# Cross network kernel, last layer: two residual additions made by accumulating GpSimd transfers onto the output, and two groups of loads made one load each

## The chip, the cores and the metric

The kernel runs on one core of a Trainium2 chip. The metric is the device time of one execution in microseconds (us), a median over several executions. The engines are called by the profile's names: PE (TensorE), DVE (VectorE), ACT (ScalarE), POOL (GpSimd) and SP (SyncE). A name with a q behind it (SPq, POOLq) is an engine's instruction queue, where DMAs are issued and semaphores are waited for.

## The reference

```python
B, D, L = 4096, 416, 6            # bf16 throughout
def reference(x0, ws, bs):        # x0 [B, D], ws [L, D, D], bs [L, D]
    x = x0
    for l in range(L):
        x = x0 * (x @ ws[l] + bs[l]) + x
    return x
```

Each of the six layers is a 4096 x 416 by 416 x 416 product, a bias, a product by element with x0 (below: the multiply) and a sum with the layer's own input (below: the add).

## The kernel before

**Layers 0 to 4** keep x transposed: features lie on the partitions, batch columns along the free axis. 416 features are three blocks of 128 (tiles XM) and a rest of 32 (tiles XR). The 4096 columns are two halves, s = 0 and 1, each of four groups of 512. PE writes into PSUM, ACT evacuates a tile of 1024 columns and adds the bias (L163), DVE multiplies by x0 (L164) and adds x (L167).

**The last layer** (from L313) swaps the operands: 128 batch rows are the stationary side, so the result comes out as rows and can be stored as it lies. For it the kernel keeps x0 as rows (X0rows, loaded by SP at L123) and the layer's input as rows (XLrows). XLrows is made near the end of layer 4 by six transposing transfers of SP (L203) for the three blocks and two ACT copies (L276) for the rest. The bias row is loaded to partitions 0, 32, 64 and 96 of bLr (L125), and a one-row matmul of ones by bLr (L334) adds it in PSUM.

The 32 row blocks of 128 rows are worked off in four rounds of eight units, a unit being one row block (L360 to L380). A round has two "quads" q and q + 1 of four units, g = 0 to 3; unit (q, g) is row block 16 s + 4 g + i, where quad q stands for (s, i). The rounds are q = 0, 2, 4 and 6. Below, u0 to u7 are the eight units of the last round: u0 to u3 are (6, 0) to (6, 3), and u4 to u7 are (7, 0) to (7, 3). For each unit PE makes three matmuls (L325) and a share of L331 and L334. The function `ew` (L345) then has

- ACT cast the PSUM result to bf16 in a tile t (L352; `tpool`, 6 buffers),
- DVE multiply t by the X0rows block in place (L353),
- the add of the unit before it done by `close_sum` (L339): DVE writes t + XLrows to a tile o (L342; `opool`, 10 buffers), and o is stored (L343),
- its own add put in the list `pending`.

So DVE's order, fixed by `keep_in_program_order`, is multiply of unit n, add of unit n - 1, multiply of unit n + 1, add of unit n, and so on. In rounds 0 and 2 and for the first pair of round 4, two row blocks go through as one instruction of 832 columns; all the other units are single, 416 columns. Stores go through SP's queue, except that of the last unit, u7, which ACT issues (L367).

POOL issues no DMA in this kernel. It fills constants and copies weights and a piece of x0 near the start (L95 to L133), and then has nothing to do. SP issues the early loads in the order of L98 to L125: the transposed x0, the weights, the four X0rows loads (L123, 832 KB each) and the four bLr loads (L125, 0.8 KB each).

Of the kernel before, what the change touches and what calls it, by code (L numbers as in the profile page):

```python
# [10 lines left out]
ALU = mybir.AluOpType  # L11
# [5 lines left out]
def kernel(  # L17
# [7 lines left out]
    nc = tc.nc  # L25
    B, D = x0.shape
    L = ws.shape[0]
    P = 128
# [4 lines left out]
    NG = 4  # L33
# [3 lines left out]
    LL = L - 1  # L37
# [7 lines left out]
    x0_v = x0.rearrange("(bt p) d -> p bt d", p=P)  # L45
    out_v = out.rearrange("(bt p) d -> p bt d", p=P)
# [8 lines left out]
    bLr = const.tile([P, D], BF16)  # L55
    bM = const.tile([P, NK, L], FP32)
    bR = const.tile([P, L], FP32)
    X0rows = big.tile([P, NBT, D], BF16)
    XLrows = big.tile([P, NBT, D], BF16)
# [10 lines left out]
    def load_wm(eng, l):  # L70
        eng.dma_start(WM[:, l], ws[l, 0:NK * P, :].rearrange("(k p) n -> p k n", p=P))
# [33 lines left out]
    for g in range(1, NG):  # L105
        dst, src = WR[32 * g:32 * g + 32, 0, :], WR[0:R, 0, :]
# [12 lines left out]
        load_wr(nc.sync, g, 1, L)  # L119
    for l in range(2, L):  # L120
        load_wm(nc.sync, l)
    for q in range(4):
        nc.sync.dma_start(X0rows[:, 8 * q:8 * q + 8, :], x0_v[:, 8 * q:8 * q + 8, :])  # L123
    for g in range(NG):
        nc.sync.dma_start(bLr[32 * g:32 * g + 1, :], bs[LL:LL + 1, :])  # L125

    def fill_wd(l0, l1):
        for g in range(NG):
# [186 lines left out]
    NQ = len(quads)  # L315
# [23 lines left out]
    def close_sum():  # L339
        while pending:  # L340
            o, t, xl, dst, eng = pending.pop()
            tc.keep_in_program_order(nc.vector.tensor_tensor(out=o, in0=t, in1=xl, op=ALU.add))  # L342
            eng.dma_start(dst, o)  # L343

    def ew(q, g0, n, src, eng):  # L345
        s, i = quads[q]
        b0 = 16 * s + 4 * g0 + i
        b = slice(b0, b0 + 4 * (n - 1) + 1, 4)
        t = tpool.tile([P, 2 * CW], BF16, name="t")
        o = opool.tile([P, 2, D], BF16, name="o")  # L350
        tv = t[:, 0:n * D].rearrange("p (a d) -> p a d", a=n)
        nc.scalar.copy(tv, src)  # L352
        tc.keep_in_program_order(nc.vector.tensor_tensor(out=tv, in0=tv, in1=X0rows[:, b, :], op=ALU.mult))  # L353
        close_sum()
        pending.append((o[:, 0:n, :], tv, XLrows[:, b, :], out_v[:, b, :], eng))
# [5 lines left out]
    for q, at, done in rounds:  # L361
        tiles = [psum.tile([P, 2, CW], FP32, tag="ps", name=f"py{n}") for n in range(4)]
        bank = [tiles[n][:, a, :] for n, a in at]

        def close(u, n):
            tl, a = at[u]
            ew(q + u // 4, u % 4, n, tiles[tl][:, a:a + n, 0:D], nc.scalar if q + 2 == NQ and u == 7 else nc.sync)  # L367

        for u in range(done):
            mm_q_full(q, u, bank[u], False)  # L370
        mm_q_rem(q, bank[0:4], done)
        close(0, done)
        mm_q_rem(q + 1, bank[4:8], 0)
        for u in range(done, 8):
            mm_q_full(q + u // 4, u % 4, bank[u], True)
            if at is not PAIRS:
                close(u, 1)
            elif u % 2:
                close(u - 1, 2)
# [31 lines left out]
```

## Time and profile before

| | |
|---|---|
| device time, median of 3 runs | 130.65 us (130.53 to 130.75) |
| the profiled execution's own time | 130.58 us |
| span of the profiled execution, first to last instruction | 128.8 us |
| granted TensorE clock | 1.000 |
| PE, DVE, ACT, POOL busy | 123.6, 106.7, 86.9, 6.2 us |
| last round: first and last matmul (start) | 119.7 and about 124.2 us |
| last round: first multiply and last add (start) | 121.20 and 125.81 us |
| issue of the last store (L343 on ACTq) | 126.22 us |

All places in time are microseconds from the span's start. "Idle before" in a row is the idle time of the engine ahead of the instruction, with what ended it. Consecutive DVE instructions overlap in the rows: the add of a single unit lasts 0.37 us, but the next instruction starts 0.28 to 0.29 us after it, and that distance is what one instruction costs when DVE has work waiting.

### The profile page before, as it was taken

How to read it: one execution, taken by the hardware profiler on the slowest of the kernel's cores; microseconds unless marked ns; L12 is line 12 of the kernel's file. 1: busy time of each engine (PE TensorE's matmuls, PEld its weight loads, DVE VectorE, ACT ScalarE, POOL GpSimd, SP SyncE). 2: the span in 40 equal slices, each digit the busy share in tenths (PEclk: the TensorE clock that was granted, in tenths of full speed). 3: DMA queues.
4: the chain of work that ended last, by engine and by line, in shares of the span. 5: the costliest groups of instructions: out<-in, count | busy, mean ns of one | idle time of the engine just before them, and what ended most of it. 6: DMA issues, size and time to landing. Idle time of an engine off the chain costs nothing.

```text
span 128.8 us, 3973 instructions
## 1 busy us (share of the span) xinstructions
PE 123.6 (96%) x1691; PEld 55.1 (43%) x1691; DVE 106.7 (83%) x195; ACT 86.9 (67%) x99; POOL 6.2 (5%) x18
## 2 busy tenths in 40 slices
PE   7999999999999999999999999999999999999960
PEld 3343443344545444434444544444444445445420
DVE  0023989999999898989898989898989899898991
ACT  0138873887848667848668848668858896569670
POOL 4004300600000000000000000000000000000000
PEclk9999999999999999999999999999999999999999
DMA  4999999999990000000000000000297999985754
GB/s 95 244 231 207 163 153 264 253 328 333 336 291 9 5 0 8 0 0 5 0 5 0 5 0 5 0 5 0 45 163 169 119 237 191 217 261 186 235 178 138
DMA packets 42102, 16.37 MB, mean 127 GB/s; under 512 B 30906, under 2 KB 42084, under 8 KB 42084
## 3 DMA queue, kind: packets, MB, share of 16 engines
q1 hardware_dynamic: 39368, 15.53, 53.9%
q10 hardware_dynamic: 2716, 0.59, 2.5%
q8 instruction: 13, 0.21, 0.7%
q14 instruction: 5, 0.04, 0.1%
HBM read 6.15 MB, written 3.41 MB: 74 GB/s over the span
## 4 chain that ended last, share of the span: by engine, by line
PE 89%; DVE 6%; issue 2%; ACT 1%; DVEq 0%
PE pt L179 49%; PE ph L212 13%; PE py L325 8%; PE pt L185 5%; PE pr L196 5%; PE wps L139 4%; DVE t L353 4%; DVE o L342 2%; PE pr L191 2%; PE ph L219 1%; PE py L331 1%; PE py L334 1%; ACT t L352 1%; PE tpr L155 0%; PE pr L155 0%
## 5 line engine op out<-in xcount | busy, mean ns | idle before, releaser
L179 PE MATMUL pt<-XM,WM 128*32 128x512 bf16 x1152 | 65.2, 379 | 0.0
L163 ACT ACTIVATE t<-pt,bM 128x1024 bf16<-128x1024 f32 x48 | 49.6, 1115 | 18.5 <-PE pt L185 18.5
L164 DVE TENSOR_TENSOR t<-t,XM 128x1024 bf16<-128x1024 bf16 x60 | 41.4, 690 | 5.2 <-ACT t L163 5.2
L167 DVE TENSOR_TENSOR XM<-t,XM 128x1024 bf16<-128x1024 bf16 x60 | 41.8, 697 | 3.4
L179 PEld LDWEIGHTS <-WM 128*32 128x32 bf16 x1152 | 29.7, 97 | 33.8 <-issue 5.1
L352 ACT CAST t<-py 128x416 bf16<-128x416 f32 (+1 forms) x23 | 14.8, 642 | 4.8 <-PE py L325 2.6
L325 PE MATMUL py<-WM,XM 128*128 128x416 bf16 x96 | 17.7, 340 | 0.0
L212 PE MATMUL ph<-XM,WM 128*128 128x512 bf16 x72 | 16.5, 381 | 0.0
L163 ACT ACTIVATE t<-ph,bM 128x1024 bf16<-128x1024 f32 x12 | 12.5, 1114 | 3.4 <-PE ph L219 3.4
L325 PEld LDWEIGHTS <-XM 128*128 128x128 bf16 x96 | 9.0, 98 | 8.5 <-issue 1.4
L353 DVE TENSOR_TENSOR t<-t,X0rows 128x416 bf16<-128x416 bf16 (+1 forms) x23 | 10.4, 457 | 1.2 <-ACT t L352 1.2
L342 DVE TENSOR_TENSOR o<-t,XLrows 128x416 bf16<-128x416 bf16 (+1 forms) x23 | 10.4, 456 | 0.0
L212 PEld LDWEIGHTS <-WM 128*128 128x128 bf16 x72 | 6.7, 98 | 8.4 <-issue 1.1
L171 ACT ACTIVATE t<-pr,bR 128x512 bf16<-128x512 f32 x10 | 6.4, 685 | 2.7 <-PE pr L196 2.1
L196 PE MATMUL pr<-XM,WM 128*32 128x512 bf16 x120 | 8.2, 379 | 0.0
L185 PE MATMUL pt<-XR,WR 32*128 32x512 bf16 x96 | 7.3, 379 | 0.0
L139 PE MATMUL wps<-const-bfloat16-1.0 128*128 128x512 bf16 (+1 forms) x12 | 4.9, 592 | 0.8 <-PEq L395 0.8
L104 ACT ACT_TABLE_LOAD x1 | 1.3, 1283 | 6.0 <-DMA XM<-in_x_dram 6.0
L173 DVE TENSOR_TENSOR XR<-t,XR 128x512 bf16<-128x512 bf16 x10 | 4.2, 425 | 0.7
L196 PEld LDWEIGHTS <-WM 128*32 128x32 bf16 x120 | 3.2, 97 | 3.0
L150 DVE CAST bM<-pb 128x18 f32<-128x18 bf16 x1 | 0.2, 177 | 5.1 <-PE pb L149 5.1
L172 DVE TENSOR_TENSOR t<-t,XR 128x512 bf16<-128x512 bf16 x10 | 4.2, 420 | 0.0
(38 smaller groups left out, 33.5 us busy)
## 6 DMA issues: line engine op xcount, KB each, us to landing
X0rows<-in_x_dram SPq DMA_DIRECT2D x4, 832.0 KB, 11.5
out_dram<-o SPq DMA_DIRECT2D x9, 208.0 KB, 2.5
WM<-in_ws_dram SPq DMA_DIRECT2D x5, 312.0 KB
out_dram<-o SPq DMA_DIRECT2D x13, 104.0 KB, 1.9
WR<-in_ws_dram SPq DMA_DIRECT2D x4, 130.0 KB, 4.1
WM<-in_ws_dram ACTq DMA_DIRECT2D x1, 312.0 KB
XM<-in_x_dram SPq DMA_TRANSPOSE x8, 4.9
xrig<-in_x_dram ACTq DMA_DIRECT2D x4, 32.0 KB, 4.2
```

What stands on the lines that cost most here:

```text
L139: nc.tensor.matmul(wps[:, 0:cols], lhsT=warm[:, 0:P], rhs=warm[:, 0:cols], start=True, stop=True)
L163: nc.scalar.activation(t[:], pt[:].rearrange("p a b -> p (a b)"), ACT.Identity, bias=bM[:, m, l:l + 1], scale=1.0)
L164: prod = nc.vector.tensor_tensor(out=t[:], in0=t[:], in1=XM[0][:, m, c0:c0 + 2 * CW], op=ALU.mult)
L167: nc.vector.tensor_tensor(out=nxt[:, m, c0:c0 + 2 * CW], in0=t[:], in1=cur[:, m, c0:c0 + 2 * CW], op=ALU.add)
L179: nc.tensor.matmul(pts[g // 2][32 * q:32 * q + 32, g % 2, :], lhsT=WM[:, l, k, 128 * m + 32 * q:128 * m + 32 * q + 32], rhs=cur[:, k, c0:c ...
L185: nc.tensor.matmul(pts[g // 2][:, g % 2, :], lhsT=WR[32 * g:32 * g + 32, l, 128 * m:128 * m + 128], rhs=curR[32 * g:32 * g + 32, CW * s:CW ...
L196: nc.tensor.matmul(pr[32 * g:32 * g + 32, :], lhsT=WM[:, l, k, NK * P:D], rhs=cur[:, k, c0:c0 + CW], start=False, stop=(k == NK - 1), tile ...
L212: nc.tensor.matmul(pt[:, gl, :], lhsT=WM[:, 0, k, 128 * m:128 * m + 128], rhs=cur[:, k, c0:c0 + CW], start=(k == 0 and not after_row), sto ...
L325: nc.tensor.matmul(py[:, 0:D], lhsT=cur[:, k, q_cols(q, g)], rhs=WM[:, l, k, :], start=((not closes) and k == 0), stop=(closes and k == NK ...
L342: tc.keep_in_program_order(nc.vector.tensor_tensor(out=o, in0=t, in1=xl, op=ALU.add))
L352: nc.scalar.copy(tv, src)
L353: tc.keep_in_program_order(nc.vector.tensor_tensor(out=tv, in0=tv, in1=X0rows[:, b, :], op=ALU.mult))
```

## The change

There are two edits.

1. **Loads.** The four X0rows loads become one load of the whole tile, and the four bLr loads become one load to partitions 0, 32, 64 and 96 from the broadcast bias row. Both stay on SP's queue at the same place.
2. **Two sums.** For the units u1 and u2 of the last round, (6, 1) and (6, 2), POOL stores the XLrows row block to the output by itself; POOL's queue gets these two transfers before the last layer's rounds are emitted. When the unit comes up, DVE's multiply writes its product to o and not back to t, and POOL issues a transfer of o to the same output rows with `accum_op=add`. The unit has no add on DVE, and no store on SP's queue; it isn't put in `pending`.

```diff
-    for q in range(4):
-        nc.sync.dma_start(X0rows[:, 8 * q:8 * q + 8, :], x0_v[:, 8 * q:8 * q + 8, :])
-    for g in range(NG):
-        nc.sync.dma_start(bLr[32 * g:32 * g + 1, :], bs[LL:LL + 1, :])
+    nc.sync.dma_start(X0rows[:], x0_v)
+    nc.sync.dma_start(bLr[0:P:32, :], bs[LL:LL + 1, :].to_broadcast([NG, D]))
...
-    def ew(q, g0, n, src, eng):
+    def rows_of(q, g0, n):
         s, i = quads[q]
         b0 = 16 * s + 4 * g0 + i
-        b = slice(b0, b0 + 4 * (n - 1) + 1, 4)
+        return slice(b0, b0 + 4 * (n - 1) + 1, 4)
+
+    ADDED = ((NQ - 2, 1), (NQ - 2, 2))
+    for q, u in ADDED:
+        b = rows_of(q, u, 1)
+        nc.gpsimd.dma_start(out_v[:, b, :], XLrows[:, b, :])
+
+    def ew(q, g0, n, src, eng):
+        b = rows_of(q, g0, n)
         t = tpool.tile([P, 2 * CW], BF16, name="t")
         o = opool.tile([P, 2, D], BF16, name="o")
         tv = t[:, 0:n * D].rearrange("p (a d) -> p a d", a=n)
         nc.scalar.copy(tv, src)
+        if (q, g0) in ADDED:
+            tc.keep_in_program_order(nc.vector.tensor_tensor(out=o[:, 0:n, :], in0=tv, in1=X0rows[:, b, :], op=ALU.mult))
+            nc.gpsimd.dma_start(out_v[:, b, :], o[:, 0:n, :], accum_op=ALU.add)
+            close_sum()
+            return
```

## The prediction

> **What bounds the kernel now.** I read the chain of work that ended last first, then the timeline of the last round, engine by engine. The page's shares of the chain say that PE carries it:
>
> ```profile
> PE 123.6 (96%) x1691; PEld 55.1 (43%) x1691; DVE 106.7 (83%) x195; ACT 86.9 (67%) x99; POOL 6.2 (5%) x18
> ...
> PE 89%; DVE 6%; issue 2%; ACT 1%; DVEq 0%
> ```
>
> But the change touches no PE work; what it may win lies where the chain is not PE. In order of time that is the stretch from 115.67 us on, DVE almost alone, and it ends so:
>
> ```profile
> 124.67 0.34 DVE t L353
> 125.02 0.09 issue
> 125.10 0.02 DVEq L342
> 125.12 0.12 issue
> 125.24 0.37 DVE t L353
> 125.62 0.29 DVE o L342
> 125.90 0.28 DVEq L406
> ```
>
> The timeline of ACT and then of DVE for the last round (start, duration) shows who feeds whom:
>
> ```profile
> 121.28 3.67 ACT L352 CAST t<-py 128x416 bf16<-128x416 f32 x7 [0.47 <-PE py L325]
> ...
> 121.82 0.38 DVE L353 TENSOR_TENSOR t<-t,X0rows 128x416 bf16<-128x416 bf16 x1
> 122.11 0.37 DVE L342 TENSOR_TENSOR o<-t,XLrows 128x416 bf16<-128x416 bf16 x1
> 122.40 0.37 DVE L353 TENSOR_TENSOR t<-t,X0rows 128x416 bf16<-128x416 bf16 x1
> ...
> 125.24 0.37 DVE L353 TENSOR_TENSOR t<-t,X0rows 128x416 bf16<-128x416 bf16 x1
> 125.53 0.66 DVE L342 TENSOR_TENSOR o<-t,XLrows 128x416 bf16<-128x416 bf16 x2
> ```
>
> The seven casts are u1 to u7. Each is 0.506 us, so their starts lie (3.67 - 0.506) / 6 = 0.527 us apart and the last ends at 124.95. DVE's multiply of u1 starts at 121.82, 0.03 after its cast ended (121.28 + 0.506 = 121.79): there DVE has just caught up with ACT. That of u7 starts at 125.24, 0.29 after its cast: DVE falls behind, because a multiply and an add cost (125.24 - 121.82) / 6 = 0.57 us a unit, 0.285 an instruction, against 0.527 from ACT. So the end of the round is set by DVE, but **ACT, with PE ahead of it, is only 0.04 us a unit faster**. PE works without a gap over 0.1 us until some 124.4, and ACT waits for nothing after 121.28.
>
> Behind the last add (start 125.81) come the store of u7 and its landing:
>
> ```profile
> 126.22 0.37 ACTq L343 DMA_DIRECT2D out_dram<-o  x1
> ...
> L406 SPq DRAIN x3: 7/7/13, 128.0 to 128.4; - x3
> ```
>
> SP has seen all stores land at 128.0, so the last takes about 1.8 us from its issue (the rows of L343 have 1.7 to 2.5 from issue to landing); the closing barrier ends the span at 128.8.
>
> **Part 1, the merged loads: nothing.** The four X0rows issues hold SP's queue from 23.28 for 7.84 us and the four bLr issues from 31.16 for 3.35 us. SP's next work is the first transposing transfers of layer 4, at 91.5 us for L203; the longest wait there is 58.2 us. The first reader of bLr is PE at 105.0, that of X0rows is DVE at 107.43, and the loads land by about 28.6 + 11.6 = 40 us. Were one load to take twice the whole stretch it would still be 40 us early, and as it is behind all other loads it can delay none. A gain is excluded as well, since SP would only wait longer.
>
> **Part 2, DVE.** Two adds go, 2 x 0.285 = 0.57 us of DVE work, but only what lies behind the last empty moment of DVE shortens the end. I walk the new order with casts ending at 121.28 + 0.527 (n - 1) + 0.506 for unit n and 0.03 us to the multiply:
> - multiply u1 121.82, add u0 122.11, multiply u2 122.40 (cast ready at 122.34): as before.
> - No add of u1. Multiply u3 waits for its cast, 122.84 + 0.03 = 122.87 (before: 122.97).
> - No add of u2, and that of u3 stands behind multiply u4. DVE idles until u4's cast, 123.37 + 0.03 = 123.40 (before: 123.54).
> - From there eight instructions follow without a gap (add u3, multiply u5, add u4, multiply u6, add u5, multiply u7, add u6, add u7): the last starts at 123.40 + 8 x 0.285 = 125.68 instead of 125.81.
>
> So **0.13 us are gained, not 0.57**: the lag before u4, three units of 0.043 us. The other 0.44 us become DVE waiting for ACT. Even an infinitely fast add ahead of u7 would leave multiply u7 at 124.98 and its add at 125.27, a gain of 0.54 us: that is the limit for any change on DVE alone.
>
> **Part 2, POOL.** Four DMA issues are new on a queue that has issued none. The first two need XLrows of half 1: the last transposing transfer is issued at 107.5 and lands 6.0 us later, 113.5. Two issues and a landing have no row on POOL. From below: the shortest store issue, 0.33 us, and 1.7 to land; from above: the longest issue of an early load, 2.48, and 2.7, the longest landing of a store. That is 113.5 + 2 x 2.48 + 2.7 = 121.2 at the latest, still before the accumulating transfers, which wait for these.
>
> The products of u1 and u2 are done at 121.82 + 0.38 = 122.20 and 122.77. The second accumulating issue stands behind the first on POOL's queue; nothing else is queued there. With an issue of g and a landing of h it is down at 122.20 + 2 g + h. With the bounds that is 124.56 (0.33, 1.7) to 129.86 (2.48, 2.7); the limit is 128.0 - 0.13 = 127.9, when the store of u7 lands. I take g = 1.14, the longest issue of a store at L343, and h = 2.5: 126.98, **0.9 us before it is needed**. So I cost it at nothing; u7's store covers it, and past g = 1.6 (with h = 2.5) it sets the end. By the Trainium skill (DMA: Bandwidth & Descriptors, Anatomy of one DMA) a GpSimd transfer of 106 KB would take 2.0 + 0.24 us, an estimate that puts it further inside; no run here shows it for an accumulating one.
>
> What else falls away: two stores on SP's queue, which kept pace with DVE anyway (SP waits for DVE ahead of nearly every one). What else is added: about 0.2 MB of stores and the accumulating traffic, at a DMA share of 0.42 to 0.68 from 114 us on; u7's store could land a little later, between 0 and 0.8 us (2.5 instead of 1.7). I take 0. At the close POOL's queue has a DRAIN of at most 0.83 us in the rows; it lies beside u7's landing.
>
> Sum against the profiled execution's own time: 130.58 - 0.13 = 130.45. That execution is 0.07 under the median, so on the median it is **130.5 us**.
>
> **Rivals.**
> (a) **POOL's transfers end last (slower).** An issue may not get on while DVE works. The traces have POOL and DVE side by side only near the start, and there they get in each other's way:
>
> ```profile
> 14.90 0.68 DVE L164 TENSOR_TENSOR t<-t,XM 128x1024 bf16<-128x1024 bf16 x1
> 15.62 0.98 DVE L167 TENSOR_TENSOR XM<-t,XM 128x1024 bf16<-128x1024 bf16 x1
> ...
> 15.00 1.06 POOL L132 COPY xrig<-xrem 128x512 bf16<-128x512 bf16 x1 [3.65 <-DMA xrem<-in_x_dram]
> ```
>
> If the accumulating issues had to wait until DVE's last add is over, 126.05, they would land at 126.05 + 2 x 0.33 + 1.7 = 128.4 up to 126.05 + 2 x 1.14 + 2.5 = 130.8, 0.5 to 2.9 us behind 127.9: 130.9 to 133.4 on the median; by the middle some 132. The point from which it decides is 127.9 us for the second landing. Slow issues alone (g = 2.48) come to 129.86, 132.5 on the median. Against it: DVE is idle in the new order before u3 and u4, just when the first issue starts. The Trainium skill (SBUF — State Buffer, two separate sides) has this as a trap: GpSimd can't write descriptors while DVE runs a 2-port mode. Its section Who interferes with whom says that an addition of two SBUF operands has no such mode and is in the way of GpSimd's reads only, inferred for descriptors. The row above, a POOL copy that reads, agrees with the second; no row shows the first. Chance 0.27.
>
> (b) **DVE is slowed by POOL (slower).** The same rows: DVE's 0.69 became 0.98 beside a POOL copy of 1.06 us; two others, beside L129's copies, took 0.80 and 0.81. If issues act likewise between 122.2 and 124.5, the instructions from multiply u4 on that fall in it (four) pay 0.11 to 0.29 each, 0.44 to 1.2, less 0.13: 130.8 to 131.7. Chance 0.10.
>
> (c) **More of the 0.57 us is realised, or the tail shortens (faster).** With two stores fewer among the last, and if DVE's own pace is better than 0.285, up to the limit of 0.54: 130.1. For it speaks little: ACT's pace stands in the row. Chance 0.21, with what lies outside the span.
>
> (d) **It doesn't do what it says:** the first two transfers come late, so that the accumulating ones wait. They would have to lose 9 us beyond 113.5; then as (a). Chance 0.02.
>
> The forecast itself keeps 0.40; its own range is 130.3 to 130.8. **Faster** by over 0.2% (0.26 us, about what a measurement of this kernel can tell from no change) is (c), 0.22 with the forecast's rim; **same** 0.40; **slower** 0.38, being (a), (b) and (d) without their rims. The range of 8 in 10 goes from 130.1, the limit of (c), to 132.0, the middle of (a).
>
> **What would show it.** Right: 21 adds in L342's row, an idle time of DVE ahead of multiply u3 and u4 put down to ACT's cast, the last add 0.1 to 0.2 us earlier, POOLq rows of L343's kind over before 125, and SP's last wait still for u7's store. Wrong: SP's or POOL's last wait for a POOL transfer (a), DVE rows above 0.37 us between 122 and 125 (b), casts closer than 0.527 us (c), or a changed difference between the execution's time and its span (now 1.8 us).

## The result, and the profile after

The changed kernel takes 131.10 us (median of 8 runs, 130.78 to 131.36) against 130.61 us before (8 runs, 130.49 to 130.75). The ratio is 1.0037, 95% interval 1.0024 to 1.0050: **slower by 0.49 us**, where 0.13 us faster was forecast. The profiled execution has 131.01 us and a span of 129.2 (129.23; before 128.81, so 0.43 longer); what lies around the span is the same 1.8 us.

First the timeline of the last round after the change, ACT and then DVE (start, duration, what). L358, L364, L360 and L340 are the cast, the multiply, the multiply of u1 and u2 into o, and the add.

```profile
121.23 3.67 ACT L358 CAST t<-py 128x416 bf16<-128x416 f32 x7 [0.47 <-DVE o L340]
...
122.35 0.37 DVE L360 TENSOR_TENSOR o<-t,X0rows 128x416 bf16<-128x416 bf16 x1
122.83 0.38 DVE L364 TENSOR_TENSOR t<-t,X0rows 128x416 bf16<-128x416 bf16 x1
123.35 0.37 DVE L364 TENSOR_TENSOR t<-t,X0rows 128x416 bf16<-128x416 bf16 x1 [0.15 <-ACT t L358]
...
125.07 0.37 DVE L364 TENSOR_TENSOR t<-t,X0rows 128x416 bf16<-128x416 bf16 x1
125.35 0.66 DVE L340 TENSOR_TENSOR o<-t,XLrows 128x416 bf16<-128x416 bf16 x2
126.04 0.38 ACTq L341 DMA_DIRECT2D out_dram<-o  x1
```

The multiplies of u3 (122.83) and u4 (123.35) now wait for their casts: the row says so for u4, and u3's starts 0.04 us after its cast has ended. The last add starts at 125.35 + 0.285 = 125.64, which is 4.41 us behind the cast of u1 (121.23); before it was 125.81 - 121.28 = 4.53. The prediction's walk through DVE's order was right to 0.01 us, and the store of u7 is issued 0.18 us earlier than before (0.05 of it because the whole last round starts that much earlier). And yet the span is longer, so the loss lies behind the last instruction that computes. The rows of the accumulating transfers, of u7's store and of the closing:

```profile
L361 POOL DMA_DIRECT2D out_dram<-o x2: 884/1048/1212, 122.4 to 123.0; - x2
...
DMA to landing us min/median/max: 2.9/3.4/3.9
...
L341 ACTq DMA_DIRECT2D out_dram<-o x1: 381/381/381, 126.0 to 126.0; - x1
...
DMA to landing us min/median/max: 2.3/2.3/2.3
...
L417 SPq DRAIN x3: 7/7/13, 128.4 to 128.7; - x3
```

The second accumulating transfer is down at about 126.9 (issued at 123.0, 3.9 to landing), which is well before the end. It is u7's own store that is late: 2.3 us from issue to landing, 2.29 by the times of the semaphore that counts the landing, where it had 1.74 before (126.22 to 127.96; the view of before has no landing row). The sum: start -0.05, DVE -0.13, landing +0.55, closing barrier +0.06 (0.90 instead of 0.84 us) make +0.43.

Why the store is late is seen in the same stretches of one microsecond of both kernels, after and then before (stretch, its length, DVE busy, clock, busy share of the DMA engines, GB/s moved; a packet counts whole in the stretch in which it starts, so a share can pass 1):

```profile
124.00:125.00 1.00, 1.00 (x5) 1.00 0.94 104
125.00:126.00 1.00, 1.00 (x4) 1.00 1.04 172
126.00:127.00 1.00, 0.01 (x1) 1.00 1.06 331
```

```profile
124.00:125.00 1.00, 1.00 (x5) 1.00 0.51 166
125.00:126.00 1.00, 1.00 (x5) 1.00 0.58 191
126.00:127.00 1.00, 0.19 (x1) 1.00 0.68 222
```

From 124 to 126 the DMA engines are full and yet move less than before: 104 GB/s at a share of 0.94, against 166 at 0.51. From 126 to 127 they move 331, which looks like a queue of stores being worked off. The packets say the same. The two accumulating transfers are 256 packets of 832 B, with a mean of 122 ns (median 88, longest 565), 31.3 us of DMA time or 1.96 us on each of the 16 engines, between 123.9 and 126.5; a plain 832 B packet of SP's stores in the last round of before takes 39 to 40 ns. Between 125.0 and 126.0 SP's queue got 101 packets through, against 261 before, and u3's store, issued at 124.04, landed 3.1 us later.

By the Trainium skill (Collectives: The Full Stack, The bandwidth ceiling: the fold count and why AG ≠ RS ≠ AR) an add on the way, in the ring collectives that it tells of, is slower than a copy because it reads two sources, about 2 times by its figures. The trace agrees that it is slower, by some 3 times in the mean (122 ns against 39) and 2.3 times in the median (88); that the second read is the reason, no run here shows.

So the first theory, T: the accumulating packets hold the DMA engines, and the last stores queue behind them. The rivals were S (POOL's transfers cost a fixed amount wherever they stand) and L (the merged loads carry the loss).

### The profile page after: what moved, and what is told of

It reads as the page before. It is cut to its first block, busy times and chain, and to the rows that moved or that the text cites. A ratio compares the mean times of both kernels' runs of the same rounds, so it can differ in the third digit from the quotient of the medians.

```text
span 129.2 us, 3968 instructions
## 1 busy us (share of the span) xinstructions
PE 123.6 (96%) x1691; PEld 55.4 (43%) x1691; DVE 106.4 (82%) x193; ACT 86.8 (67%) x99; POOL 9.1 (7%) x22
## 4 chain that ended last, share of the span: by engine, by line
PE 94%; DVE 2%; ACT 0%; issue 0%; DVEq 0%
PE pt L177 49%; PE ph L210 13%; PE py L323 12%; PE pt L183 5%; PE pr L194 5%; PE wps L137 4%; PE pr L189 2%; PE ph L217 1%; PE py L329 1%; PE py L332 1%; DVE t L364 1%; DVE o L340 1%; ACT t L358 0%; PE pr L153 0%; DVEq L417 0%
## 5 line engine op out<-in xcount | busy, mean ns | idle before, releaser
L358 ACT CAST t<-py 128x416 bf16<-128x416 f32 (+1 forms) x23 | 14.7, 641 | 4.8 <-PE py L323 2.1
L364 DVE TENSOR_TENSOR t<-t,X0rows 128x416 bf16<-128x416 bf16 (+1 forms) x21 | 9.7, 465 | 1.5 <-ACT t L358 1.4
L340 DVE TENSOR_TENSOR o<-t,XLrows 128x416 bf16<-128x416 bf16 (+1 forms) x21 | 9.6, 463 | 0.0
L351 POOL DMA_DIRECT2D out_dram<-XLrows x2 | 1.3, 642 | 87.8 <-DMA XLrows<-XM 87.8
```

## The experiments

All ratios are to the kernel before, from runs on the same chip, with 95% intervals.

**The parts one by one.** e1 has the merged loads alone:

```diff
-    for q in range(4):
-        nc.sync.dma_start(X0rows[:, 8 * q:8 * q + 8, :], x0_v[:, 8 * q:8 * q + 8, :])
-    for g in range(NG):
-        nc.sync.dma_start(bLr[32 * g:32 * g + 1, :], bs[LL:LL + 1, :])
+    nc.sync.dma_start(X0rows[:], x0_v)
+    nc.sync.dma_start(bLr[0:P:32, :], bs[LL:LL + 1, :].to_broadcast([NG, D]))
```

Expected: 

> Only the merged loads of the change, no sums moved. Theory T (the accumulating packets, which hold a DMA engine 122 ns each against 36 for a plain one, hold up the last stores): ratio to before 1.000 +- 0.001. Rival L (the merged loads carry the loss): 1.003 to 1.004. Rival S (POOL's DMAs cost about 0.4 us wherever they stand): 1.000.

Measured: 131.33 us, **1.0062** (1.0047 to 1.0078). This was a surprise: the merged loads alone cost 0.8 us, more than the whole change, and no accumulating transfer is in the kernel. The row of u7's store:

```profile
L341 ACTq DMA_DIRECT2D out_dram<-o x1: 372/372/372, 126.3 to 126.3; - x1
...
DMA to landing us min/median/max: 2.3/2.3/2.3
```

e2 is the change without the merged loads (the same lines the other way round).

Expected: 

> Only the two sums by accumulating transfers, the loads as before. T and S: ratio about 1.0035, the landing of u7's store 2.2 to 2.4 us after its issue. L: 0.999 to 1.000.

Measured: 131.42 us, 1.0074 (1.0056 to 1.0092), u7's landing 2.52 us after its issue. As L and T can't both be the whole, and 0.0062 + 0.0074 is far from 0.0037, none of the three theories was enough.

e3 leaves the two adds out (two row blocks of the output lack the layer's input) and stores the products by SP:

```diff
-            nc.gpsimd.dma_start(out_v[:, b, :], o[:, 0:n, :], accum_op=ALU.add)
+            eng.dma_start(out_v[:, b, :], o[:, 0:n, :])
```

Expected: 

> The adds of u1 and u2 are left out altogether: their products are stored by SP as plain stores, so that two row blocks lack the layer's input; no POOL transfer, loads as before. If the step of 0.13 us is right and whole: ratio 0.999, last add 0.13 us earlier relative to the casts, landing of u7's store 1.7 to 1.8 us as before (T and S alike). If a DVE that ends earlier does not shorten the end: 1.000.

Measured: 130.49 us, 0.9996 (0.9988 to 1.0005). The last add starts 4.41 us behind the cast of u1, as in after, and u7's store lands 1.72 us after its issue. The gain on DVE is there in the trace. In the time it isn't shown: a step of 0.13 us would be 0.9990, and the interval holds that value and 1 alike.

e4 moves the two accumulating transfers 3 us ahead, all else as after:

```diff
-    ADDED = ((NQ - 2, 1), (NQ - 2, 2))
+    ADDED = ((NQ - 4, 3), (NQ - 3, 0))
```

Expected: 

> As after, but the two accumulating transfers are those of units (4, 3) and (5, 0) in round 4, about 3 us earlier. T: their packets are over before u3's store, the last landing is again 1.7 to 1.8 us after its issue, no DVE gain at the end as DVE catches up with ACT at u1 anyway: ratio 1.000 to 1.001 (0.06 us of longer closing barrier). S: 1.003 to 1.004. L: 1.003 to 1.004.

Measured: 130.68 us, 1.0012 (1.0004 to 1.0021). The accumulating packets are as slow as before (mean 121 ns) but over by 123.4, and u7's store lands 1.78 us after its issue:

```profile
L341 ACTq DMA_DIRECT2D out_dram<-o x1: 372/372/372, 126.5 to 126.5; - x1
...
DMA to landing us min/median/max: 1.8/1.8/1.8
```

T holds: it is the collision with the last stores that costs. Of S no more is left than 0.16 us (0.05 to 0.27), a little over what was expected; 0.05 of it is the closing barrier.

**What the merged loads do.** In e1 DVE ends as in before (u7's store is issued at 126.25, before 126.22), no POOL transfer is in flight, and still u7's store lands 2.31 us after its issue. The waits of SP in the tail of before and then of e1 (engine, line, waited for: us in total, times, longest):

```profile
SPq L406 <- DMA out_dram<-o: 1.4, 4, 0.5
```

```profile
SPq L404 <- DMA out_dram<-o: 2.0, 1, 2.0
```

In before, SP's closing waits are met one after the other as the stores land; in e1 there is a single long one. I then listed SP's instructions with their times in every kernel, semaphore waits among them, and looked for a place where SP is late without a reason in the program. There is one, at the same count in each: **SP's instruction 79** (the first is 0) starts 0.44 to 0.47 us after the one ahead of it has ended, where SP's other instructions need 0.03 to 0.06 when they wait for nothing and the neighbouring stores start 0.14 to 0.23 behind. Some 0.6 to 0.8 us after its start (1.4 in e2) a packet of 8192 B runs in the queue that the profile calls "instruction":

```profile
q14 instruction: 5, 0.04, 0.1%
```

Which instruction is number 79 depends only on how many stand ahead of it. The merged loads take six away, and the two POOL sums four more. So this table, worked out from the instruction, packet and landing records of each trace (the kernels from e5 on are told below):

```
kernel     SP's 79th is       8 KB packet   u7's store: issue  landing   us    last part*   ratio
before     u2's store         124.55        126.22  127.96    1.74    0.04
e1         u5's store         126.43        126.25  128.56    2.31    0.40    1.0062
e5         u1's store         124.04        126.20  127.92    1.72    0.03    1.0007
e9         u5's store         126.25        126.17  128.72    2.55    0.66    1.0069
after      a closing wait     127.41        126.04  128.33    2.29    0.21    1.0037
e2         u4's store         126.25        126.04  128.56    2.52    0.18    1.0074
e10        a store of round 4 121.60        126.03  128.25    2.23    0.18    1.0027
e4         a closing wait     127.66        126.46  128.24    1.78    0.00    1.0012
e7         a closing wait     127.43        126.22  127.95    1.73    0.04    1.0012
e3         u2's store         124.25        125.98  127.70    1.72    0.02    0.9996
e11        a wait in round 4  122.16       126.10  127.84    1.74    0.02    0.9998
e12        a wait in round 4  122.18       126.07  127.84    1.77    0.01    0.9994
* a store counts its landing in 16 parts: time from the 15th to the last
```

Theory F: at its instruction 79 SP stops for some 0.4 us and has more of its instructions fetched, which is the 8 KB packet, and when both fall on the last stores the kernel ends later. (That the packet is a fetch for SP is read from the queue's name and from its place behind instruction 79 in every trace. It runs after that instruction has started, so it isn't what that instruction waited for.)

In e1 the excess has three pieces. The late instruction delays u5's and u6's stores, so that 15 of the 16 parts of u7's land at 128.16 and not at 127.92. The last part comes 0.40 us behind them, about the 0.43 us of the 8 KB packet; in e9 below it is 0.66 and 0.65. From 127.5 on the last packets of SP's and of u7's stores end in turn, one about every 0.04 us, as on a single DMA engine that has fallen behind, until 127.91; before, u7's are over at 127.56. That this engine is the one that carried the 8 KB packet is argued from the sizes only, since a packet's record doesn't name its engine.

The third piece isn't F's: u7's landing is no longer the last of SP's closing waits, so that three more waits of 0.06 us follow it, 0.17 us in all. Those three are there in e5 and e9 too, and two of them in e2.

The Trainium skill (Runtime: NRT & Kernel Launch, Instruction fetch mechanics) says that an engine's sequencer fetches its next block of instructions by its own DMA queue and that crossing into it is mostly hidden. Here it is hidden where instruction 79 starts 2.3 us (before) or 2.9 us (e5) ahead of the last store's issue; at u5's store, 0.6 us ahead (e1, e9), it isn't.

e5 tests F against L: e1 with eight loads more that nobody needs, so that instruction 79 moves ahead.

```diff
     nc.sync.dma_start(bLr[0:P:32, :], bs[LL:LL + 1, :].to_broadcast([NG, D]))
+    pad = const.tile([1, 8, 32], BF16)
+    for n in range(8):
+        nc.sync.dma_start(pad[0:1, n, :], bs[0:1, 32 * n:32 * n + 32])
```

Expected: 

> The merged loads alone, plus eight loads of 64 bytes into a tile that nothing reads, put on SP's queue behind them (SP's instruction 79, counted from 0, is late by 0.44 to 0.47 us in every trace so far, and an 8 KB transfer of the instruction queue follows some 0.7 us later; eight more instructions move it from u5's store to u1's). Theory F (the place of that instruction in the tail is what the merged loads cost): ratio 1.000 to 1.002, instruction 79 is u1's store. Rival L (the merged loads themselves cost): 1.006 again.

Measured: 130.71 us, **1.0007** (0.9999 to 1.0016). Adding eight needless loads to e1 makes it 0.6 us faster, and u7's store lands 1.72 us after its issue instead of 2.31. The merged loads themselves cost nothing that the time shows (the trace has the 0.17 us of closing waits); it is the count of instructions that costs.

e6 was to show the same without a merged load, with two X0rows and the four bLr loads issued by POOL:

```diff
-    for q in range(4):
+    for q in range(2):
         nc.sync.dma_start(X0rows[:, 8 * q:8 * q + 8, :], x0_v[:, 8 * q:8 * q + 8, :])
-    for g in range(NG):
-        nc.sync.dma_start(bLr[32 * g:32 * g + 1, :], bs[LL:LL + 1, :])
...
     fill_wd(1, L)
+    for q in range(2, 4):
+        nc.gpsimd.dma_start(X0rows[:, 8 * q:8 * q + 8, :], x0_v[:, 8 * q:8 * q + 8, :])
+    for g in range(NG):
+        nc.gpsimd.dma_start(bLr[32 * g:32 * g + 1, :], bs[LL:LL + 1, :])
```

Expected: 

> No merged load and no moved sum: six of the eight early loads (two of X0rows, four of bLr) are only issued by POOL instead of SP, so that SP has six instructions fewer, as with the merged loads. F: instruction 79 is u5's store, ratio 1.005 to 1.007. L: 1.000. A third possibility, that POOL transfers cost something wherever they stand: 1.001 or so by the early-accumulation run.

Measured: 135.77 and 136.85 us in the two fastest of six runs, 1.0439 (the other four took 140.3 to 144.2). This edit spoilt something else. In POOL's queue the first of these loads came to stand ahead of the copies, as its timeline shows:

```profile
10.91 1.04 POOL L133 DMA_DIRECT2D X0rows<-in_x_dram  x1
...
18.27 0.61 POOL L130 COPY xrig<-xrem 128x512 bf16<-128x512 bf16 x1 [6.06 <-DMA xrem<-in_x_dram]
```

832 KB that are needed at 107 us now run at the same time as the small load of xrem, which lands at 18 instead of 15 us, and PE waits for it in the first layer. The time says nothing on F. (Its tail does agree: number 79 is u5's store, and u7's lands 2.39 us after its issue.)

e9 does it in a place where nothing waits: three stores of round 0 go to POOL as plain stores, which takes six instructions from SP's queue; loads and sums are as before.

```diff
+            eng = nc.sync
+            if q + 2 == NQ and u == 7:
+                eng = nc.scalar
+            elif q == 0 and u in (0, 2, 4):
+                eng = nc.gpsimd
-            ew(q + u // 4, u % 4, n, tiles[tl][:, a:a + n, 0:D], nc.scalar if q + 2 == NQ and u == 7 else nc.sync)
+            ew(q + u // 4, u % 4, n, tiles[tl][:, a:a + n, 0:D], eng)
```

Expected: 

> The loads and all sums as before; only three stores of round 0, 13 us before the end, are issued by POOL as plain stores, so that SP has six instructions fewer ahead of its tail, as with the merged loads. Theory F: instruction 79 is u5's store, u7's store lands 2.2 to 2.4 us after its issue, ratio 1.003 to 1.007. If the place of instruction 79 is not what costs: 0.999 to 1.001, as plain POOL stores cost nothing in the run with them.

Measured: 131.56 us, **1.0069** (1.0055 to 1.0082). u7's store of e9 and its landing, and the closing:

```profile
L343 ACTq DMA_DIRECT2D out_dram<-o x1: 373/373/373, 126.2 to 126.2; - x1
...
DMA to landing us min/median/max: 2.5/2.5/2.6
...
L411 SPq DRAIN x3: 7/7/7, 129.0 to 129.3; - x3
```

u7's landing, 2.55 us after its issue, is later than the 2.2 to 2.4 that were expected. The three stores had landed by 114.7, some 15 us before the end; with no merged load and nothing of the last round touched, the end is 0.9 us later. F stands: e1 and e9 have nothing in common but the six instructions and the three closing waits behind u7's, and e5, which has the waits alone, has no loss that the time shows.

**What the accumulating transfers do, by themselves.** e7 keeps the merged loads and lets POOL store the finished rows of u1 and u2 plainly, with the adds on DVE:

```diff
+            eng = nc.sync
+            if q + 2 == NQ and u == 7:
+                eng = nc.scalar
+            elif q + 2 == NQ and u in (1, 2):
+                eng = nc.gpsimd
-            ew(q + u // 4, u % 4, n, tiles[tl][:, a:a + n, 0:D], nc.scalar if q + 2 == NQ and u == 7 else nc.sync)
+            ew(q + u // 4, u % 4, n, tiles[tl][:, a:a + n, 0:D], eng)
```

Expected: 

> Merged loads as in after, both adds back on DVE, and the finished rows of u1 and u2 stored by POOL as plain stores. SP's instruction 79 falls among the closing waits, as in after. Theory T (accumulating packets are the slow ones): POOL's packets take 36 to 45 ns, the last landing is 1.7 to 1.9 us after its issue, ratio 0.999 to 1.001. Rival Q (any POOL store among the last ones holds up the others): landing 2.2 us or more, ratio 1.003 to 1.005.

Measured: 130.73 us, 1.0012 (1.0003 to 1.0020), landing 1.73 us; the ratio is just above the expected 0.999 to 1.001. POOL's plain packets are 64 of 2496 and 4160 B, larger than I had expected, and take 9.7 us of DMA time together, or 38 ns for each 832 B; the accumulating ones needed 31.3 us for the same 208 KB. The stretches of e7 show it: more is moved at a smaller share.

```profile
124.00:125.00 1.00, 1.00 (x5) 1.00 0.30 107
125.00:126.00 1.00, 1.00 (x5) 1.00 0.92 306
126.00:127.00 1.00, 0.19 (x1) 1.00 0.59 192
```

e8 doubles the dose:

```diff
-    ADDED = ((NQ - 2, 1), (NQ - 2, 2))
+    ADDED = ((NQ - 2, 1), (NQ - 2, 2), (NQ - 2, 3), (NQ - 1, 0))
```

Expected: 

> As after, but four accumulating transfers, u1 to u4. T: 512 packets of 122 ns are 62 us of DMA engine time, 3.9 us on each of 16 from about 123.9 on, so the last store lands 1.5 to 2.5 us later than in after, though DVE's last add is 0.1 to 0.3 us earlier: ratio 1.013 to 1.025. If the accumulating transfers do not hold up the stores: at most 1.004.

Measured: 133.59 us, **1.0230** (1.0216 to 1.0244). 512 packets of 123 ns, 3.93 us on each engine, until 128.8; u7's store, issued at 125.91 and so the earliest of all kernels, lands 3.8 us later. Its timeline, DVE and then POOL (start, duration, what), and the row of u7's store:

```profile
125.23 0.66 DVE L340 TENSOR_TENSOR o<-t,XLrows 128x416 bf16<-128x416 bf16 x2
...
122.40 3.58 POOL L361 DMA_DIRECT2D out_dram<-o  x4 [6.56 <-DVE o L340]
...
L341 ACTq DMA_DIRECT2D out_dram<-o x1: 372/372/372, 125.9 to 125.9; - x1
...
DMA to landing us min/median/max: 3.8/3.8/3.8
```

e10 takes F away from the two sums: e2 with ten needless loads on SP's queue (as in e5), so that instruction 79 lies ahead of the tail.

Expected: 

> The two accumulating transfers of the change with the loads as before, and ten 64-byte loads on SP's queue, so that instruction 79 lies at some 121 us, ahead of the tail, and u7's store has the last place in SP's closing waits, as in before. T alone is left: last landing 2.1 to 2.3 us after its issue, ratio 1.002 to 1.004 (1.0074 without the ten loads). If the accumulating transfers cost nothing once instruction 79 is out of the way: 0.999 to 1.000.

Measured: 130.90 us, 1.0027 (1.0016 to 1.0037), landing 2.23 us. This is T alone; after, where number 79 falls among the closing waits, has 1.0037 (1.0024 to 1.0050), not told apart from it. And e2, with T and F both, had 1.0074; 0.13 us of the difference to e10 are e2's two closing waits behind u7's.

e11 and e12 accumulate one unit only, with the loads as before and nine needless loads, e11 u1 and e12 u2:

```diff
-    ADDED = ((NQ - 2, 1), (NQ - 2, 2))
+    ADDED = ((NQ - 2, 2),)
```

Expected of e11: 

> One accumulating transfer, u1's, loads as before, nine 64-byte loads on SP's queue. T: 128 packets, some 1 us on each DMA engine, over by about 125.3, u7's landing 1.75 to 1.9 us after its issue; DVE's last add 0.09 us earlier: ratio 0.999 to 1.001.

Expected of e12: 

> One accumulating transfer, u2's, loads as before, nine 64-byte loads. By the walk through DVE's order, leaving out the add of u2 alone gives the whole 0.13 us, because DVE is empty ahead of u4 either way. T: the packets run from about 124.2 to 125.5, u7's landing 1.75 to 2.0 us after its issue: ratio 0.9985 to 1.001. Should it come out below 0.9995, this is a version that beats both kernels.

Measured: e11 130.51 us, 0.9998 (0.9988 to 1.0008); e12 130.50 us, **0.9994** (0.9985 to 1.0003). DVE in e12 (the row x2 at 122.94 is the multiplies of u3 and u4):

```profile
122.94 0.81 DVE L369 TENSOR_TENSOR t<-t,X0rows 128x416 bf16<-128x416 bf16 x2
...
125.10 0.37 DVE L369 TENSOR_TENSOR t<-t,X0rows 128x416 bf16<-128x416 bf16 x1
125.38 0.65 DVE L345 TENSOR_TENSOR o<-t,XLrows 128x416 bf16<-128x416 bf16 x2
126.07 0.37 ACTq L346 DMA_DIRECT2D out_dram<-o  x1
```

The last add starts 4.41 us behind the cast of u1 (121.26), the same as with two adds less: as DVE is empty ahead of u4 in either case, the add of u1 that the change took away had bought nothing, and its transfer cost 128 packets. The packets of one transfer are over by 125.7, and u7's store lands 1.77 us after its issue. e12 beats the changed kernel. That it beats the kernel before isn't shown, since its interval includes 1.

## Why the prediction was wrong

- **DVE (0.13 us gained, not 0.57): right.** After, e3 and e12 all have the last add 4.41 us behind the cast of u1 and not 4.53, and DVE waits for the casts of u3 and u4. That the time follows isn't shown: e3 (0.9996) and e12 (0.9994) lean that way, but both intervals include 1.
- **POOL's issues and when the sums are down: right in the sum, and partly by luck.** The second landing came at 126.92, where 126.98 was forecast and 127.9 was the limit. But the first issue started 0.25 us later than taken, the two (0.88 and 1.21 us) overlapped and held POOL for 1.78 us instead of 2 x 1.14, and the landing came 2.69 us after the second issue's end instead of 2.5: the errors cancel.
- **The step that failed: "u7's store could land a little later, between 0 and 0.8 us (2.5 instead of 1.7). I take 0."** It measured 0.55 us later in after, more than the whole loss of 0.43 in the span. I asked when the accumulating transfers would be down, and not how long their packets would hold the DMA engines that the last stores need. The share of the DMA engines before, about 0.5 from 123 us on, looked like room, but it is room for plain packets of 38 or 39 ns; these took 122 ns and filled it for two microseconds. e4, e7 and e8 show that it is these packets and their place.
- **The merged loads at nothing: right for the loads, wrong for the queue.** "SP would only wait longer" is true at 31 us. But six instructions fewer move SP's instruction 79 by three units in the tail: alone that costs 0.8 us (e1, 0.17 of it in closing waits), and moving it by needless loads gives that back to within what the time can tell (e5). In the change it helps: with ten instructions fewer in all, number 79 falls behind the last store, among the waits. Without the merged loads the change would have been at 1.0074 and not at 1.0037. The prediction had no term for this, because in the trace of before it costs nothing: SP is late there at u2's store, 2.3 us before the last one, and catches up.
- **Rival (a)**, POOL's transfers end last: didn't happen; SP's last wait is still for u7's store. **Rival (b)**, DVE slowed by POOL: didn't happen either. DVE's rows beside the two POOL issues (122.4 to 124.2) are 0.37 and 0.38 us, as before, and the issues went on beside a busy DVE. Of the two rules of the Trainium skill that were weighed there (SBUF — State Buffer), the one of Who interferes with whom, by which (inferred there) additions with two SBUF operands don't keep GpSimd from writing descriptors, is the one that the traces agree with. **Rival (c)**, more gain: e3 and e12 exclude all but 0.2 us of it. **(d)** didn't happen: the first two transfers had landed by 118.6.
- **The range.** 131.10 lies inside 130.1 to 132.0, but the range reached up there for rival (a), which didn't happen: that is luck. Two of the lower bounds don't come out of the prediction's own terms: (a)'s 130.9 (130.5 + 0.5) and (b)'s 130.8 (130.65 + 0.44 - 0.13) should both be 131.0. Neither touches the sum or the range.

**What stays open.** Of the 0.6 us by which u7's landing is late in e1 (0.75 in e9), how much comes from SP's delay and how much from the 8 KB packet wasn't tried apart; the parts of the landing suggest 0.24 and 0.36. Nor is it shown why accumulating packets differ so much in length (median 88 ns, longest 565).

## What to carry to other kernels

Ask of a transfer that is "hidden" not only when it lands but what it occupies meanwhile: here an accumulating store took three times the DMA time of a plain one, and it stood ahead of the store that ends the kernel. In the last microseconds a free engine isn't worth much if its release adds work to the shared one; look where DVE waits again, and take off only the add whose removal brings the instructions behind that wait forward (here one, u2's, and not two). And when an edit far from the end moves the time by half a per cent, count the instructions on the queue that issues the last stores, before explaining it by what the edit does.

## What the runs showed of the hardware that was not expected

- SP's instruction 79 starts 0.44 to 0.47 us after the end of the one ahead in all fourteen traces, whatever that instruction is, and a packet of 8192 B of the instruction queue, of 0.31 to 0.66 us, follows. At u5's store it makes u7's landing 0.6 to 0.75 us later (e1, e9); 2.3 us and more ahead of u7's issue it costs nothing that shows (before, e5).
- Two accumulating stores of 104 KB each from POOL: 256 packets of 832 B, mean 121 to 131 ns (after, e2, e4, e10); the same rows as plain POOL stores (e7): 64 packets, 38 ns for each 832 B.
- POOL's issue of an accumulating store took 0.88 and 1.21 us in after, and 0.90, 1.24, 1.57 and 1.91 us for the four of e8, which start 0.53 to 0.57 apart and overlap; landing came 2.9 and 3.9 us after the issue's start in after. Plain POOL issues took 0.54 to 0.72 us (after, e7), landing 4.1 and 4.3 us after the issue's start among the stores of rounds 0 and 2 (after), and 2.1 and 2.2 in the last round (e7). u7's plain store by ACT has 0.37 and 1.74 us before.
- SP works its closing waits off in order, at some 0.06 us for each that is already met; behind u7's landing stood none in before, three in e1, e5 and e9.
- With POOL transfers in the kernel the closing barrier is 0.04 to 0.06 us longer (0.88 to 0.90 us in after, e4, e7 and e10, against 0.84 in before and e3).
